# An attention and feed-forward kernel: one buffer for squares and sums, sums of weights made over three chunks, and a matmul of zeros in each product visit

## The chip, the cores and the metric

One core of a Trainium2 chip runs the whole program. The metric is the time on the device in microseconds. The engines are named as in the profile: PE is TensorE's matmuls and PEld its weight loads, DVE is VectorE, ACT is ScalarE, POOL is GpSimd, SP issues DMAs.

## The reference

Attention with a window and with block summaries, then a feed-forward layer with a squared relu. Sizes: batch 4, 8 heads, 768 positions, head size 64; 3072 tokens of 512 features, 2048 hidden features.

```python
def attn(q, k, v):                      # block = 32, window = 16
    k_sum = k.reshape(B, H, nb, block, D).max(axis=3)
    v_sum = v.reshape(B, H, nb, block, D).mean(axis=3)
    scores_l = scale * q @ k.T          # kept where |i - j| < window, else -1e9
    scores_s = scale * q @ k_sum.T + log(block)
    a = softmax(concat(scores_l, scores_s))
    return a @ concat(v, v_sum)

def ffn(x, w_in, w_out):                # x: attention output, (3072, 512)
    h = maximum(x @ w_in, 0)
    return (h * h) @ w_out
```

## The kernel before

The tokens are worked off in 12 chunks of 256. A list of tokens (`START`) orders the first two chunks and the preparation of the weights; from chunk 2 on `period` writes the order out, chunk by chunk, in 8 slots. The program is not reordered: each engine takes its instructions in the order in which they are issued.

Every matmul keeps float32 accuracy by splitting each operand into a high part, rounded to float32r, and a low part, the rest; a product is high x high + high x low + low x high, three matmuls. Weights are split once, activations as they come.

In slot n of chunk c PE runs `ffn1_pair`: the first layer for two blocks of 128 hidden features, 24 matmuls of 128 x 256 into one PSUM bank `ph`. Then it runs `second` for the slot before: the second layer for the four 128 x 128 blocks of squares. While PE does that and the next slot's first layer, the other engines turn `ph` into squares and their high and low parts, `gh` and `gl` (two buffers, by slot parity). So PE comes back to a slot's squares one first layer and one second layer after their bank is full.

From chunk 3 on, seven of the eight pairs use a product scheme with 7 instead of 8 block products (`products`, 21 matmuls of 128 x 256; a plain visit, as for pair 0 and in chunk 2, is 12 of 128 x 512). It needs sums of blocks of squares (`squares_and_sums`: four differences on VectorE, L443 to L449) and sums of blocks of `w_out`, made once (`build`, in five steps: six additions on GpSimd over four steps, then two casts on ScalarE and two subtractions on VectorE). The sums of pairs 1, 3, 5 and 7 don't fit: they are written to DRAM and read back a little before each use (`stream`). Four PSUM banks gather the products; `open_banks` starts them with matmuls of zeros, and `evict_products` adds them up at the chunk's end.

`BUILDS` says in which slot each step of a build is issued: "b" ahead of the slot's squares, "m" after them, "a" after the attention's middle part. In each slot L400 makes the relu on ScalarE, L406 squares three blocks there (high part, plain), L440 makes the product on VectorE in place, L447 the plain low part on GpSimd, L443, L448 and L449 the sums in a buffer of their own, L453 their high part on ScalarE and L454 their low part on GpSimd. In plain slots L411 and L414 do product and low part on VectorE.

Attention for the next chunk's two groups of 128 positions is laid over the slots: scores in slots 0 and 3, the masked maximum (`mask_max`), exponentials on ScalarE, `inverse` on VectorE and `norm` on GpSimd in slots 1, 2 and 4, 5, transposes (`turn`, L343, 12 a group) on VectorE in slots 2, 3 and 5, 6, outputs (L361, 64 matmuls) in slot 7. The second group's outputs need its last four transposes, which stand on VectorE behind slot 6's product and sums. Chunks 3, 4, 6 and 7 also carry the block sums of the next batch's K and V, chunks 2, 5 and 8 put the summary of V in place.

Of the kernel before, what the change touches and what calls it, by code (L numbers as in the profile page):

```python
# [11 lines left out]
F32 = mybir.dt.float32  # L12
# [12 lines left out]
P = 128  # L25
# [12 lines left out]
STREAMED = (1, 3, 5, 7)  # L38
BUILDS = {
# [40 lines left out]
def attn_ffn_kernel(ctx: ExitStack, tc: tile.TileContext, q, k, kt, v, vt, v0, w, masks, ident, mean, out):  # L80
# [24 lines left out]
    r_sb = const.tile([P, DM], F32, name="r")  # L105
    s_sb = const.tile([P, DM], F32, name="s")
# [189 lines left out]
    def mask_max(g, h):  # L296
# [4 lines left out]
        if half not in nmx:  # L301
            nmx[half] = work.tile([P, 4], F32, name="nmx", tag="nmx", bufs=7)
            sm[half] = work.tile([P, 4], F32, name="sm", tag="sm", bufs=7)
# [124 lines left out]
    def squares(ph, k):  # L428

        r = relu(ph, r_sb, nc.scalar)  # L430
        high_square(flat(gh_sb, k), r)
        square(ph, r)
        low_square(flat(gl_sb, k), ph, flat(gh_sb, k))

    def squares_and_sums(ph, k):

        r = relu(ph, r_sb, nc.scalar)
        o = slice(0, 3 * P)
        high_square(gh_sb[:, k, o], r[:, o])
        nc.vector.tensor_mul(out=r, in0=ph, in1=r)  # L440
        a12, a22, a11, a21 = (r[:, i * P : (i + 1) * P] for i in range(4))
        s1, s3, s2, s4 = (s_sb[:, i * P : (i + 1) * P] for i in range(4))
        nc.vector.tensor_sub(  # L443
            out=s_sb[:, 0 : 2 * P].rearrange("p (a b) -> p a b", a=2), in0=a21.unsqueeze(1).to_broadcast([P, 2, P]),
            in1=r[:, P : 3 * P].rearrange("p (a b) -> p a b", a=2),
        )
        nc.gpsimd.tensor_sub(out=gl_sb[:, k, o], in0=r[:, o], in1=gh_sb[:, k, o].bitcast(F32))  # L447
# [143 lines left out]
    def slot(c, n, before, mid, after, last):  # L591
# [29 lines left out]
        if summed:  # L621
            split_sums(k)
# [242 lines left out]
```

## Time and profile before

| | |
|---|---|
| median of 3 runs | 667.4 us (666.64 to 669.68) |
| the profiled execution | 667.81 us, its span 666.0 us |
| TensorE matmul, weight load | 609.5 us (92%), 567.6 us (85%) |
| VectorE | 510.1 us (77%) |
| ScalarE | 291.6 us (44%) |
| GpSimd | 277.9 us (42%) |
| mean granted TensorE clock | 0.974 of full speed |

The times of the rows are of the profiled execution and count from its span's start. The busy time of a matmul overlaps that of its neighbours, so a busy share says little of how fast they follow each other; starts do.

### The profile page before, as it was taken

To read this page: it belongs to the slowest core of one execution; us is meant where nothing else is said; L and a number is where in the kernel's file an instruction comes from. 1 tells how busy PE (TensorE), PEld (TensorE's weight loads), DVE (VectorE), ACT (ScalarE), POOL (GpSimd) and SP (SyncE) were. 2 spreads that over 40 slices of the span, in tenths; PEclk is the share of its full clock that TensorE was granted. 3 is DMA by queue.
4 is the path that set the end of the run, shared out by engine and by line. 5 is a ranking of instruction groups with operands and counts; after the bars stand their busy time and mean duration, and the time that the engine had idled before them with its cause. 6 is when DMAs were issued, how large, how long until landed. Compare 5 with 4: busy or idle time off the path is not lost.

```text
span 666.0 us, 14839 instructions
## 1 busy us (share of the span) xinstructions
PE 609.5 (92%) x5859; PEld 567.6 (85%) x5859; DVE 510.1 (77%) x1240; ACT 291.6 (44%) x748; POOL 277.9 (42%) x252
## 2 busy tenths in 40 slices
PE   3689999999989788998999998998998999999997
PEld 2578888988878788998988998988998998998897
DVE  4898998957756876787787788788698588588554
ACT  3678685224444333443443443443434444443232
POOL 3635462005637662442453343343254244244242
PEclk9789999999989977999999999998999999999999
DMA  8689311550216421732621732732532432331410
GB/s 337 215 351 376 116 64 48 184 189 1 88 58 200 171 96 65 237 111 96 215 88 48 238 112 96 230 120 74 186 104 83 138 132 82 127 97 48 155 67 33
DMA packets 27638, 91.15 MB, mean 137 GB/s; under 512 B 3376, under 2 KB 3504, under 8 KB 25520
## 3 DMA queue, kind: packets, MB, share of 16 engines
q1 hardware_dynamic: 27568, 90.20, 39.2%
q8 instruction: 46, 0.75, 0.5%
q14 instruction: 24, 0.20, 0.1%
HBM read 80.75 MB, written 9.44 MB: 135 GB/s over the span
## 4 chain that ended last, share of the span: by engine, by line
PE 39%; DVE 38%; ACT 12%; issue 5%; POOL 4%; DMA 1%; DVEq 0%; SPq 0%; ACTq 0%; POOLq 0%
PE ph L392 17%; DVE pT L343 8%; DVE s L443 8%; PE zw L522 6%; ACT e_sb L312 5%; DVE r L440 4%; PE o_ps L463 4%; PE o_ps L522 4%; PE o_ps L586 3%; ACT r L400 2%; DVE s L448 2%; DVE s L449 2%; ACT gh L406 2%; DVE e_sb L304 2%; DVE w_sb L263 1%
## 5 line engine op out<-in xcount | busy, mean ns | idle before, releaser
L392 PE MATMUL ph<-xh,w_sb 128*128 128x256 f32 x1408 | 251.9, 281 | 2.0 <-DVE gl L414 1.1
L392 PEld LDWEIGHTS ph<-xh,w_sb 128*128 128x128 f32 x1408 | 215.9, 189 | 8.2 <-issue 2.7
L392 PE MATMUL ph<-xl,w_sb 128*128 128x256 f32 x704 | 197.1, 280 | 0.2
L392 PEld LDWEIGHTS ph<-xl,w_sb 128*128 128x128 f32 x704 | 132.8, 189 | 1.6 <-DVE xl L377 1.6
L447 POOL TENSOR_TENSOR gl<-r,gh 128x384 fp32r<-128x384 f32 x63 | 64.5, 1024 | 150.4 <-DVE r L440 145.7
L453 ACT CAST gh<-s 128x512 fp32r<-128x512 f32 x63 | 39.1, 621 | 181.2 <-DVE s L449 171.6
L454 POOL TENSOR_TENSOR gl<-s,gh 128x512 fp32r<-128x512 f32 x63 | 81.9, 1300 | 76.2 <-issue 58.4
L343 DVE STREAM_TRANSPOSE pT<-e_sb 32x256 f32<-32x256 f32 x228 | 99.4, 436 | 3.3
L400 ACT ACTIVATE r<-ph 128x512 f32<-128x512 f32 x85 | 50.3, 592 | 84.1 <-PE ph L392 36.7
L312 ACT ACTIVATE e_sb<-e_sb,nmx 128x120 f32<-128x120 f32 x192 | 73.5, 384 | 25.9 <-DVE nmx L304 25.9
L330 POOL TENSOR_TENSOR e_sb<-e_sb,sm 128x480 f32<-128x480 f32 x43 | 43.3, 1008 | 96.2 <-DVE sm L325 88.6
L443 DVE TENSOR_TENSOR s<-r 128x256 f32<-128x256 f32 x63 | 75.4, 1197 | 6.5
L440 DVE TENSOR_TENSOR r<-ph,r 128x512 f32<-128x512 f32 x63 | 43.5, 691 | 37.5 <-ACT gh L406 30.3
L406 ACT ACTIVATE gh<-r 128x384 fp32r<-128x384 f32 (+1 forms) x96 | 54.0, 562 | 20.5 <-PE o_ps L463 12.9
L522 PE MATMUL zw<-sums,gh 128*128 128x256 f32 x252 | 51.5, 286 | 0.7 <-ACT gh L453 0.6
L522 PE MATMUL zw<-w_sb,gh 128*128 128x256 f32 x252 | 51.7, 287 | 0.3 <-ACT gh L406 0.3
L522 PE MATMUL o_ps<-w_sb,gh 128*128 128x256 f32 x252 | 50.3, 281 | 0.0
L256 POOL TENSOR_TENSOR w_raw<-w_raw 128x1024 int32<-128x1024 int32 x16 | 34.2, 2147 | 37.0 <-DVE w_raw L251 13.9
L304 DVE CUSTOM_DVE_ANT_0 e_sb<-s_ps,mask_sb 128x120 f32<-128x120 f32 x192 | 42.6, 274 | 8.2 <-PE s_ps L292 5.8
L586 PE MATMUL o_ps<-w_sb,gh 128*128 128x512 f32 x144 | 46.1, 402 | 0.2 <-ACT gh L406 0.2
L411 DVE TENSOR_TENSOR ph<-ph,r 128x512 f32<-128x512 f32 x25 | 17.4, 695 | 33.6 <-ACT r L400 33.3
L522 PEld LDWEIGHTS zw<-sums,gh 128*128 128x128 f32 x252 | 39.5, 194 | 2.0 <-ACT gh L453 2.0
(119 smaller groups left out, 1165.4 us busy)
## 6 DMA issues: line engine op xcount, KB each, us to landing
sums<-sums SPq DMA_DIRECT2D x40, 768.0 KB, 4.8
w_raw<-in_w SPq DMA_DIRECT2D x16, 1024.0 KB, 10.2
v_sb<-in_v SPq DMA_DIRECT2D x24, 384.0 KB, 6.7
k_sb<-in_k SPq DMA_DIRECT2D x18, 384.0 KB, 5.4
q_sb<-in_q SPq DMA_DIRECT2D x24, 256.0 KB, 5.5
out<-ob SPq DMA_DIRECT2D x22, 256.0 KB, 2.1
kv<-in_kt SPq DMA_DIRECT2D x8, 384.0 KB, 3.2
kv_sb<-in_kt SPq DMA_DIRECT2D x8, 384.0 KB, 4.0
```

The source lines that it names most:

```text
L304: nc.vector.tensor_tensor_reduce(out=e_sb[:, h, 0:NK], in0=s_ps[g][h % 2][:, h // 2, 0:NK], in1=m, scale=-scale, scalar=3.0e38, op0=ALU.ad ...
L312: nc.scalar.activation(e, e, AF.Exp, bias=nmx[half][:, i : i + 1], scale=-1.0, accum_out=sm[half][:, i : i + 1])
L343: nc.vector.transpose(out=pT[g % 2][j * 32 : j * 32 + 32, :, i * 32 : i * 32 + 32], in_=e_sb[i * 32 : i * 32 + 32, :, j * 32 : j * 32 + 32],)
L392: nc.tensor.matmul(ph, lhsT=w_sb[f][:, w, cc * P : (cc + 1) * P], rhs=x[c][:, cc, :], start=(n == 0), stop=(n == 3 * NC4 - 1))
L400: nc.scalar.activation(r, ph, AF.Relu)
L406: nc.scalar.activation(gh, r, AF.Square)
L440: nc.vector.tensor_mul(out=r, in0=ph, in1=r)
L443: nc.vector.tensor_sub(out=s_sb[:, 0 : 2 * P].rearrange("p (a b) -> p a b", a=2), in0=a21.unsqueeze(1).to_broadcast([P, 2, P]), in1=r[:, P ...
L447: nc.gpsimd.tensor_sub(out=gl_sb[:, k, o], in0=r[:, o], in1=gh_sb[:, k, o].bitcast(F32))
L454: nc.gpsimd.tensor_sub(out=gl_sb[:, k, o], in0=s_sb, in1=gh_sb[:, k, o].bitcast(F32))
L522: nc.tensor.matmul(bank[n_ps][:, o], lhsT=g_[:, k, blk * P : (blk + 1) * P], rhs=b[:, w], start=False, stop=(n == 2 and (n_ps, o.start) in ...
L586: nc.tensor.matmul((X, Y)[tt], lhsT=g_[tt], rhs=w_sb[2 * p + i][:, w, DM:], start=(begins and i == 0 and m == 0), stop=(ends and i == 1 an ...
```

## The change

Squares and sums share one buffer `r_sb` of seven blocks, and the relu has its own, `h_sb`. The product is no longer made in place: it writes four blocks of `r_sb`, with a gap for two sums. All seven blocks get their high part by one cast on ScalarE and their low part by one subtraction on GpSimd (`split`), issued after the middle part of the attention. The square on ScalarE and the plain low part go. Plain slots do the same with four blocks. The product visit first takes the 14 matmuls with high parts of squares, then the 7 with low parts, and begins with a matmul of zeros on 8 columns. The builds of the seven sums are issued over chunks 2 (pairs 1, 2, 3), 3 (5, 7) and 4 (4, 6), each with its last step ahead of the next slot's squares; pairs 4 and 6 stay plain in chunk 3. `nmx` has 6 buffers instead of 7, and the DMA scratch is 512 instead of 1024.

```diff
@@ -36,14 +36,14 @@
 FROM_KT = 6
 NP = NF // 2
 STREAMED = (1, 3, 5, 7)
+PRODUCTS_FROM = {1: 3, 2: 3, 3: 3, 5: 3, 7: 3, 4: 4, 6: 4}
 BUILDS = {
-    2: [(2, "a", 1, 0), (2, "a", 1, 1), (3, "b", 1, 2), (3, "b", 1, 3), (3, "a", 1, 4)]
-    + [(4, "b", 2, 0), (4, "b", 2, 1), (4, "a", 2, 2), (4, "a", 2, 3), (5, "b", 2, 4)]
-    + [(5, "a", 3, 0), (5, "a", 3, 1), (6, "b", 3, 2), (6, "b", 3, 3), (6, "a", 3, 4)]
-    + [(7, "b", 4, 0), (7, "b", 4, 1), (7, "a", 4, 2), (7, "a", 4, 3)],
-    3: [(0, "b", 4, 4), (0, "a", 5, 0), (0, "a", 5, 1), (0, "a", 5, 2), (0, "a", 5, 3), (1, "a", 5, 4)]
-    + [(2, "b", 7, 0), (2, "b", 7, 1), (3, "b", 7, 2), (3, "b", 7, 3), (3, "a", 7, 4)]
-    + [(4, "b", 6, 0), (4, "b", 6, 1), (5, "b", 6, 2), (5, "b", 6, 3), (5, "a", 6, 4)],
+    c: [(n, "a", p, step) for p, at in pairs for step, n in enumerate(at)] + [(at[3] + 1, "b", p, 4) for p, at in pairs]
+    for c, pairs in {
+        2: ((1, (1, 1, 2, 2)), (2, (3, 3, 4, 4)), (3, (5, 5, 6, 6))),
+        3: ((5, (1, 2, 2, 3)), (7, (4, 4, 5, 5))),
+        4: ((4, (1, 2, 2, 3)), (6, (4, 4, 5, 5))),
+    }.items()
 }
 LAST_ORDER = (2, 1, 4, 3, 6, 5, 7, 0)
 MASKED = -1.0e9
@@ -102,8 +102,8 @@
     pT = [const.tile([P, H, P], F32, name=f"pT{i}") for i in range(2)]
     ksums = [const.tile([P, NPAIR, NB], F32, name=f"ksum{i}") for i in range(2)]
     vsum = const.tile([P, NPAIR, 32], F32, name="vsum")
-    r_sb = const.tile([P, DM], F32, name="r")
-    s_sb = const.tile([P, DM], F32, name="s")
+    h_sb = const.tile([P, DM], F32, name="h")
+    r_sb = const.tile([P, 7 * P], F32, name="r")
     gh_sb = const.tile([P, 2, 7 * P], F32R, name="gh")
     gl_sb = const.tile([P, 2, 7 * P], F32R, name="gl")
     xh_sb = const.tile([P, NPAIR, CT], F32R, name="xh")
@@ -299,7 +299,7 @@
         m = mask_sb[:, 0 if t == 0 else 2 if t == NT - 1 else 1, :]
         half, i = divmod(h, 4)
         if half not in nmx:
-            nmx[half] = work.tile([P, 4], F32, name="nmx", tag="nmx", bufs=7)
+            nmx[half] = work.tile([P, 4], F32, name="nmx", tag="nmx", bufs=6)
             sm[half] = work.tile([P, 4], F32, name="sm", tag="sm", bufs=7)
         nc.vector.tensor_tensor_reduce(
             out=e_sb[:, h, 0:NK], in0=s_ps[g][h % 2][:, h // 2, 0:NK], in1=m, scale=-scale, scalar=3.0e38,
@@ -427,31 +427,27 @@
 
     def squares(ph, k):
 
-        r = relu(ph, r_sb, nc.scalar)
-        high_square(flat(gh_sb, k), r)
-        square(ph, r)
-        low_square(flat(gl_sb, k), ph, flat(gh_sb, k))
+        h = relu(ph, h_sb, nc.scalar)
+        nc.vector.tensor_mul(out=r_sb[:, 0:DM], in0=ph, in1=h)
+        return lambda: split(k, DM)
 
     def squares_and_sums(ph, k):
 
-        r = relu(ph, r_sb, nc.scalar)
-        o = slice(0, 3 * P)
-        high_square(gh_sb[:, k, o], r[:, o])
-        nc.vector.tensor_mul(out=r, in0=ph, in1=r)
-        a12, a22, a11, a21 = (r[:, i * P : (i + 1) * P] for i in range(4))
-        s1, s3, s2, s4 = (s_sb[:, i * P : (i + 1) * P] for i in range(4))
-        nc.vector.tensor_sub(
-            out=s_sb[:, 0 : 2 * P].rearrange("p (a b) -> p a b", a=2), in0=a21.unsqueeze(1).to_broadcast([P, 2, P]),
-            in1=r[:, P : 3 * P].rearrange("p (a b) -> p a b", a=2),
+        h = relu(ph, h_sb, nc.scalar)
+        r = r_sb.rearrange("p (a b) -> p a b", b=P)
+        nc.vector.tensor_mul(
+            out=r_sb[:, 0 : 6 * P].rearrange("p (a b) -> p a b", a=2)[:, :, 0:CT],
+            in0=ph.rearrange("p (a b) -> p a b", a=2), in1=h.rearrange("p (a b) -> p a b", a=2),
         )
-        nc.gpsimd.tensor_sub(out=gl_sb[:, k, o], in0=r[:, o], in1=gh_sb[:, k, o].bitcast(F32))
-        nc.vector.tensor_sub(out=s2, in0=a11, in1=s1)
-        nc.vector.tensor_sub(out=s4, in0=a12, in1=s2)
-
-    def split_sums(k):
-        o = slice(3 * P, 7 * P)
-        nc.scalar.copy(out=gh_sb[:, k, o], in_=s_sb)
-        nc.gpsimd.tensor_sub(out=gl_sb[:, k, o], in0=s_sb, in1=gh_sb[:, k, o].bitcast(F32))
+        nc.vector.tensor_sub(out=r[:, 2:5:2], in0=r[:, 4:5].to_broadcast([P, 2, P]), in1=r[:, 1:4:2])
+        nc.vector.tensor_sub(out=r[:, 5], in0=r[:, 3], in1=r[:, 2])
+        nc.vector.tensor_sub(out=r[:, 6], in0=r[:, 0], in1=r[:, 5])
+        return lambda: split(k, 7 * P)
+
+    def split(k, n):
+        gh = gh_sb[:, k, 0:n]
+        nc.scalar.copy(out=gh, in_=r_sb[:, 0:n])
+        nc.gpsimd.tensor_sub(out=gl_sb[:, k, 0:n], in0=r_sb[:, 0:n], in1=gh.bitcast(F32))
 
     X, Y, Z, W = bank[6], bank[7], bank[2], bank[3]
 
@@ -470,7 +466,7 @@
         return [[g_[:, k, b * P : (b + 1) * P] for b in FIRST[i]] for g_ in (gh_sb, gl_sb)]
 
 
-    built, sums = set(), {}
+    sums = {}
     dram = {p: tc.dram_tile([P, 1536], F32, name=f"sums{p}") for p in STREAMED}
 
     def halves(f, m):
@@ -502,7 +498,6 @@
         nc.vector.tensor_sub(out=b12[:, 1], in0=t1, in1=b12[:, 0].bitcast(F32))
         if p in STREAMED:
             nc.sync.dma_start(out=dram[p].rearrange("p (h c) -> p h c", h=2), in_=t.bitcast(F32))
-        built.add(p)
 
     def stream(p, tag_room=True):
         t = room(F32R, "sums")[:, 0:1536] if tag_room else shared(F32R, "sums")
@@ -514,10 +509,13 @@
         t3, t4, t2 = (sums[p][:, :, i * CT : (i + 1) * CT] for i in range(3))
         t1, b11, b21, b22 = halves(2 * p, 1), halves(2 * p, 0), halves(2 * p + 1, 0), halves(2 * p + 1, 1)
         lo, hi = slice(0, CT), slice(CT, DM)
-        plain = (2, b11, 2, lo), (0, b21, 6, lo), (1, t4, 7, lo)
-        summed = (4, t3, 3, lo), (3, t1, 3, hi), (5, t2, 2, hi), (6, b22, 6, hi)
-        passes = [(m, n) for m in plain for n in range(3)] + [(m, n) for m in summed for n in range(2)]
-        for (blk, b, n_ps, o), n in passes + [(m, 2) for m in summed]:
+        plain = (3, b11, 2, lo), (0, b21, 6, lo), (1, t4, 7, lo)
+        summed = (4, t3, 3, lo), (2, t1, 3, hi), (5, t2, 2, hi), (6, b22, 6, hi)
+        passes = [(m, n) for ms in (plain, summed) for m in ms for n in range(2)]
+        nc.tensor.matmul(
+            Z[:, 0:8], lhsT=zero.to_broadcast([P, P]), rhs=zero.to_broadcast([P, 8]), start=False, stop=False
+        )
+        for (blk, b, n_ps, o), n in passes + [(m, 2) for m in plain + summed]:
             g_, w = ((gh_sb, 0), (gh_sb, 1), (gl_sb, 0))[n]
             nc.tensor.matmul(
                 bank[n_ps][:, o], lhsT=g_[:, k, blk * P : (blk + 1) * P], rhs=b[:, w],
@@ -569,15 +567,20 @@
     def order(c):
         return LAST_ORDER if c == n_c - 1 else range(NP)
 
+    def in_products(c, p):
+        return c >= PRODUCTS_FROM.get(p, n_c)
+
     def second(c, n):
 
         p, k = order(c)[n], n % 2
         begins, ends = n == 0, n == NP - 1
-        summed = c > 2
-        if summed and begins:
+        if begins and c > 2:
             open_banks(*((Z, W) if p == 0 else (X, Y, Z, W)))
-        if p in built:
-            products(p, k, ((2, CT), (3, CT), (6, CT), (7, 0)) if ends else ((2, CT), (3, CT)) if n == NP - 2 and c == n_c - 1 else ())
+        if in_products(c, p):
+            closes = ((6, CT), (7, 0)) if ends else ()
+            if not any(in_products(c, later) for later in list(order(c))[n + 1 :]):
+                closes += ((2, CT), (3, CT))
+            products(p, k, closes)
             return
         for tt in range(TPC):
             for i in range(2):
@@ -604,8 +607,7 @@
             scores(a + 1, 0, NPAIR)
         for do in before:
             do()
-        summed = c > 2 and p > 0
-        (squares_and_sums if summed else squares)(ph, k)
+        rest = (squares_and_sums if in_products(c, p) else squares)(ph, k)
         if n == NP - 1 and a < n_g:
             for g in (a, a + 1):
                 high_x(g)
@@ -618,8 +620,7 @@
                 evict(c - 1, NF - 1, tt, nc.scalar)
         for do in mid:
             do()
-        if summed:
-            split_sums(k)
+        rest()
         for do in after:
             do()
         for do in last:
@@ -631,14 +632,12 @@
         before, mid, after, last = steps = [[[] for _ in range(8)] for _ in range(4)]
         for n, where, p, step in BUILDS.get(c, ()):
             steps["bmal".index(where)][n].append(lambda p=p, step=step: build(p, step))
-        if c > 2:
-            last[0].append(lambda: stream(1))
-            last[2].append(lambda: stream(3))
-            last[4].append(lambda: stream(5))
-            if c < n_c - 1:
-                last[6].append(lambda: stream(7))
-            else:
-                last[1].append(lambda: stream(7, False))
+        for p in STREAMED:
+            if in_products(c, p):
+                if c == n_c - 1 and p == 7:
+                    last[1].append(lambda: stream(7, False))
+                else:
+                    last[p - 1].append(lambda p=p: stream(p))
         a = 2 * c + 2
         b, t = divmod(a, NT)
         if a >= n_g:
@@ -761,7 +760,7 @@
             o = FIRST[j][0] * P
             ffn1(c, 2 * f + j, ph_of[i][:, o : o + CT])
         elif op == "RE":
-            r_of[i] = relu(ph_of[i], r_sb, eng)
+            r_of[i] = relu(ph_of[i], h_sb, eng)
         elif op == "SQ":
             g_of[i] = [high_square(flat(gh_sb, i % 2), r_of[i])]
         elif op == "MU":
@@ -852,7 +851,7 @@
     arrays["masks"] = _masks()
     arrays["ident"] = np.eye(P, dtype=np.float32)
     arrays["mean"] = _mean()
-    nc = bacc.Bacc("TRN2", target_bir_lowering=False, num_devices=1, dynamic_dma_scratch_size=1024)
+    nc = bacc.Bacc("TRN2", target_bir_lowering=False, num_devices=1, dynamic_dma_scratch_size=512)
     args = [
         nc.dram_tensor(f"in_{n}", a.shape, mybir.dt.from_np(a.dtype), kind="ExternalInput").ap()
         for n, a in arrays.items()
```

## Rows read from the trace of the kernel before

**Rows 1.** Windows by chunk: us, length, busy of each engine, clock, DMA share, GB/s.

```profile
202.98:266.72 63.74, 54.36 (x483) 50.91 (x482) 49.09 (x107) 24.24 (x66) 35.46 (x35) 0.89 0.37 130
266.72:318.92 52.20, 48.89 (x484) 46.30 (x482) 42.35 (x109) 21.18 (x60) 19.99 (x18) 1.00 0.42 142
318.92:370.30 51.38, 49.39 (x484) 46.29 (x482) 40.66 (x109) 21.04 (x60) 21.95 (x21) 1.00 0.35 114
370.30:421.25 50.95, 48.16 (x483) 46.00 (x482) 41.43 (x107) 21.15 (x60) 19.96 (x18) 1.00 0.43 146
421.25:474.20 52.95, 49.69 (x483) 47.38 (x482) 42.34 (x109) 21.18 (x60) 19.97 (x18) 0.97 0.41 140
...
525.58:574.61 49.03, 47.90 (x483) 45.83 (x482) 38.62 (x103) 21.04 (x60) 20.00 (x18) 1.00 0.37 119
574.61:623.67 49.06, 47.00 (x451) 45.00 (x449) 38.50 (x101) 21.86 (x61) 22.29 (x20) 1.00 0.28 89
```

**Rows 2.** Order of time on PE, chunk 10: start, length, line, count, idle.

```profile
608.20 1.15 PE L361 MATMUL ph<-pT,v_sb 128*64 128x64 f32 x32
609.18 0.64 PE L361 MATMUL s_ps<-pT,v_sb 128*64 128x64 f32 x16
610.79 0.69 PE L361 MATMUL s_ps<-pT,v_sb 128*64 128x64 f32 x16 [0.98 <-DVE pT L343]
```

**Rows 3.** Order of time, other engines, slots 6 and 7 of chunk 10.

```profile
606.19 0.69 DVE L440 TENSOR_TENSOR r<-ph,r 128x512 f32<-128x512 f32 x1
...
606.96 1.02 POOL L447 TENSOR_TENSOR gl<-r,gh 128x384 fp32r<-128x384 f32 x1 [2.21 <-DVE r L440]
...
606.98 1.27 DVE L443 TENSOR_TENSOR s<-r 128x256 f32<-128x256 f32 x1
...
608.62 0.29 DVE L449 TENSOR_TENSOR s<-r,s 128x128 f32<-128x128 f32 x1
608.94 1.80 DVE L343 STREAM_TRANSPOSE pT<-e_sb 32x256 f32<-32x256 f32 x4
608.94 0.62 ACT L453 CAST gh<-s 128x512 fp32r<-128x512 f32 x1 [4.56 <-DVE s L449]
...
609.69 1.27 POOL L454 TENSOR_TENSOR gl<-s,gh 128x512 fp32r<-128x512 f32 x1 [1.72 <-issue]
```

**Rows 4.** The order of time on DVE in chunk 3.

```profile
237.32 0.43 DVE L443 TENSOR_TENSOR s<-r 128x256 f32<-128x256 f32 x1
```

**Rows 5.** Waits of PE in chunk 3: total us, times, longest.

```profile
PE zw L522 <- POOL gl L447: 4.5, 2, 2.7
```

**Rows 6.** Groups by shape, whole span: busy us, mean ns, idle before.

```profile
L330 POOL TENSOR_TENSOR e_sb<-e_sb,sm 128x480 f32<-128x480 f32 x43 | 43.3, 1008 | 96.2 <-DVE sm L325 88.6 <-ACT r L400 7.2 <-ACT gh L406 0.4
...
L487 POOL TENSOR_TENSOR ob<-w_sb 128x512 f32<-128x512 f32 x14 | 18.1, 1315 | 15.5 <-DMA out<-ob 8.3 <-DVE w_sb L502 7.0 <-POOL ob L487 0.2
...
L263 POOL TENSOR_TENSOR w_sb<-w_raw,w_sb 128x1024 fp32r<-128x1024 f32 x3 | 7.6, 2535 | 2.4 <-ACT w_sb L137 2.3
...
L200 DVE TENSOR_REDUCE vsum<-kv_sb 128x24 f32<-128x768 f32 x8 | 7.5, 937 | 0.1
...
L499 ACT CAST sums<-ob 128x768 fp32r<-128x768 f32 x7 | 5.8, 833 | 12.1 <-POOL ob L495 12.1
```

**Rows 7.** Windows of PE: two runs of 24 matmuls in chunk 11.

```profile
627.96:630.69 2.73, 2.73 (x26) 1.00 0.85 249
633.07:635.90 2.83, 2.83 (x26) 1.00 0.82 341
```

**Rows 8.** Waits of PE in chunk 2.

```profile
PE s_ps L361 <- DVE pT L343: 2.7, 1, 2.7
```

**Rows 9.** DMA issues of the page: count, KB each, us to landing.

```profile
sums<-sums SPq DMA_DIRECT2D x40, 768.0 KB, 4.8
```

**Rows 10.** Weight loads by line: count, minimum, median, maximum ns.

```profile
L522 PEld LDWEIGHTS zw<-w_sb,gh x252: 186/188/337, 208.8 to 658.0; 128*128 128x128 f32 x126
...
L361 PEld LDWEIGHTS ph<-pT,v_sb x352: 132/138/138, 44.0 to 609.1; 128*64 128x64 f32 x176
```

## The prediction

> **What bounds the kernel now.** I read the windows by chunk first [rows 1]: from chunk 3 on each row is the stretch between two first uses of the opened banks, with the busy time of each engine. The reader is to see that TensorE is busy for nearly all of it, and that chunks doing the same matmuls still differ: 49.0 us for chunks 9 and 10, 51 to 53 for 5 to 8 (chunk 8 as chunk 5), 63.7 for chunk 3. What differs is waiting, so the question is who is waited for. Then the order of time on TensorE at the end of chunk 10 [rows 2]: of the 64 matmuls of the two attention outputs 48 run, and the last 16 sit 0.98 us until VectorE's transposes `pT` are there; from the step of the matmuls before it, the next one would have come 1.2 us earlier. This wait is in every chunk with attention. Then VectorE, ScalarE and GpSimd at that moment [rows 3]: VectorE goes without a pause from the product of one slot to its four transposes, and its broadcast subtraction (L443) takes 1.27 us. Its engine is not slow: in chunk 3 the same instruction takes 0.43 us [rows 4]. At 606.96 GpSimd's L447 begins, at 606.98 L443 does, and it ends one subtraction's length after GpSimd's end: it stood behind GpSimd for 0.84 us. So in the attention half of a chunk VectorE sets the end, TensorE elsewhere, and in chunk 3 GpSimd, whose sums of weights hold up the low parts (4.5 us in two waits, [rows 5]).
>
> **The change, part by part.** My unit is a slot; T is the end of its first-layer matmuls.
>
> *VectorE's relief.* L447 disappears. GpSimd's one subtraction now waits for the cast, the cast for the last of VectorE's three, so the three meet no subtraction of their own slot; and they can't meet that of the slot before, because the product writes the buffer which it reads and so waits for its end. L443 falls from 1.27 to 0.43 us. The product also no longer waits for ScalarE's square, since it doesn't overwrite what the square reads.
>
> The Trainium skill, "SBUF — State Buffer", section "Who interferes with whom", says that a VectorE instruction with two SBUF inputs and a GpSimd instruction that reads SBUF exclude each other for a whole instruction. The 1.27 against 0.43 agrees with that. By this rule a 2.15 us subtraction is also a longer block than the 1.0 us one was for whatever still meets it.
>
> What still meets it is the first operation of the softmax inverse, in slots 2 and 5; I take that in below.
>
> *The new ring.* Product, subtractions, cast, GpSimd, next product follow each other through one buffer. Product to next instruction 0.79 (606.19 to 606.98); the first subtraction 0.43 and a gap of 0.03; from its end at 608.25 to the end of the last 0.66, less that gap: 1.88 [rows 3, 4]. Cast of 896: 512 take 0.62 [rows 3], 768 take 0.833 [rows 6], so 0.94; I take 0.95. From the cast's end to GpSimd 0.13 [rows 3]. GpSimd's 896: by the step from 384 to 512 (1.02 to 1.27, [rows 3]) 2.02; by the line from 512 to 1024 (1.315 and 2.535, [rows 6]) 2.23; I take 2.15, between them. With 0.13 for two semaphores the ring is 5.23 us. TensorE's bare slot is 24 and 21 matmuls at 0.114 us [rows 7], 5.12, with the 22nd 5.22. They are level: the ring costs nothing where it is 5.23 and 0.1 us a bare slot where it is 5.33. Bare slots are four in each of chunks 5 to 10 and seven in the last, 31.
>
> *The chunk that results.* Slot 4: relu done at T+0.85, product T+0.95, sums T+2.8, cast to T+3.8; GpSimd's normalization (1.0 us, [rows 6]) goes first, its subtraction ends at T+6.5, and TensorE wants the low parts at 5.22 for the slot and 15 matmuls more, T+6.9. Slot 5: the inverse waits for GpSimd (0.4), sums at T+8.95, cast to T+9.95 (wanted T+10.4), subtraction to T+12.2 (wanted T+12.2, no slack left), eight transposes to T+12.5. Slot 6: sums T+14.4, four transposes (1.80, [rows 3]) T+16.2; TensorE reaches the 49th output matmul at T+16.5. The 1.2 us wait is gone: 49.05 becomes 47.85. With the sum of V in slot 5 of chunks 6 and 7 (0.94 us on VectorE, [rows 6], and some 0.3 with its scaling) 0.8 us stay: 48.6. Where V is placed (chunks 5 and 8) I take 48.1. Six chunks: 2 x 47.85 + 2 x 48.6 + 2 x 48.1 = 289.1 against 304.75 [rows 1]: **-15.7 us**. Chunk 7's 53.0 holds a spell of the half clock after its waits (0.97 mean granted clock, [rows 1]); I let it go with them.
>
> *Sums of weights.* A build is two adds of 1.315 [rows 6] and four of half as many elements, some 5.5 us of GpSimd, then two casts on ScalarE (768 elements 0.833, 256 by the same step 0.4) and two VectorE operations. Chunk 3 had nearly three, chunk 4 none; now both have two, behind the slot's subtraction instead of ahead of it. But the casts stand ahead of the next relu on ScalarE, and wait for GpSimd's last add. In slot 4 this puts the relu some 3.7 us late, and everything queued behind it: 3.4 us until the cast, 0.9 for the low part. Slot 5, with two adds, a normalization and 2.15 on GpSimd: 1.3 and 0.5. Slot 6, relu late again: the first outputs wait 2.6 for a bank, the last 1.9 for transposes. Together 10.6 us a chunk, and about 2 for the clock that falls in such waits (0.89 mean in chunk 3, [rows 1]). Chunk 3 also makes two visits plain, 0.4 each. 2 x (47.85 + 10.6 + 2) + 0.8 = 121.7 against 115.9: **+5.8 us**. Bounds: at the old chunk 3's price, 14.7 over 49.0 for three builds, it would be near 0 or below, -4 if spreading helps; with chunk 3's waits in both, +11. Chunk 2 had 3.7 us of waits, 2.7 of them for transposes [rows 8], and a clock spell of 1; its three builds now cost 3.9 by the same reckoning. Its low part moves from VectorE to GpSimd (1.3), at T+3.8 where it is wanted at T+5.9, so it costs nothing alone, and what it would cost behind an add is in the 3.9: **-0.8**. The DMAs of the sums move with them; at 4.8 us from issue to landing [rows 9] for the write and again for the read, group 7's come back some 2 us before chunk 4 uses them, group 5's about when slot 6 does; SP's loads of q, k and v stand behind them, a chunk ahead of their use.
>
> *Last chunk.* Its opening of banks waits for VectorE's evictions, which come 1.2 us sooner; its end waits longer, because the last plain visit has product, cast and GpSimd (1.3) in a row instead of a square beside a product, +1.5: **+0.3**.
>
> *The 22nd matmul.* Eight columns, so its price is the weight load of 128 columns. A load of 128 columns shows 188 ns, one of 64 shows 138 [rows 10]: 50 ns for 64, about 0.1 us for 128. From 0 (if it hides in a wait) to 0.114, a full step; I take 0.105, for 61 visits: 6.4. What it can return: the same 24 matmuls take 2.73 us in one slot and 2.83 in the next [rows 7], 0.114 or 0.118 a step, and in undisturbed stretches the step changes with each visit of 21, as if it went by whether the number of matmuls so far is even. In chunk 2, whose visits have 12, it is always the fast one. 1230 of 3003 recorded matmuls in chunks 3 to 11 are slow; with 22 all could be fast: 1230 x 0.0044 = 5.4 us. Net **+1.0**.
>
> Sum: -15.7 + 5.8 - 0.8 + 0.3 + 1.0 = -9.4. The profiled execution took 667.8 us (its span 666.0, 1.8 around it), the median of the runs is 667.4; so **658 us**.
>
> **Rivals.** *The step doesn't follow the count.* Waits inside visits already shift it, against the rule; then the zeros cost 6.4 and return nothing: 663.5. If all stay slow, 7 us more. 0.13. *Spreading the sums pays* (-4 instead of +5.8): 648. For it: the waits of rows 5 come from adds ahead of a low part, and adds now stand behind it. 0.14. *The relief is hidden:* normalization or inverse behind 2.15 us of GpSimd makes the transposes as late as today; six times 1.2 come back, 665. Against it: 0.3 us in slot 6 by my times. 0.09. *The ring sets the slot, and the kernel is slower:* the wait of the product for GpSimd. Each 0.1 us over 5.23 costs 31 x 0.1 = 3.1; at 5.53 the gain is gone, from 5.64 on it is slower than before by over 0.5%; with the subtractions still 0.84 longer, in their new strided form or behind other GpSimd work, it is 6.1 and 684. Against it: nothing of GpSimd is left to meet them in a bare slot. 0.09, middle 674.
>
> **How the numbers follow.** My forecast has 0.55, and 652 to 664 as its own range (the bounds of GpSimd's 896, 0.1 us on 31 slots, and of the zeros). The range of 646 to 668 takes in the spread sums, the unpaid zeros and the hidden relief, and leaves the ring and a still better case out. Half a per cent, about what a measurement of this kernel tells from no change, is 3.3 us. Faster by more, below 664: 0.52 of the forecast's 0.55, 0.14, 0.08 of the zeros' 0.13, 0.01 elsewhere: 0.75. Within: 0.17, the hidden relief and the rest of the forecast and of the zeros, with some ring. Slower: 0.08, nearly all ring.
>
> **What would show it.** L443's successor at 0.43 us; no pause at the 49th output matmul in chunks 9 and 10, which last under 48.5 with the zeros; GpSimd's 896 at 2.0 to 2.25 and a product that starts just after it in the last chunk; 24 matmuls in 2.73 us everywhere; long relus' waits in slots 4 and 6 of chunks 3 and 4. Wrong if visits begin with a wait for the cast in bare slots, or if chunks 3 and 4 together leave 112 to 127 us.

## The result, and the profile after

The changed kernel takes 650.64 us, median of 4 runs (649.25 to 651.41), against 668.1 (666.64 to 669.68) beside it: ratio 0.9736 [0.9705, 0.9766]. Forecast were 658.0 and a gain of 9.4; measured is one of 17.5. The profiled span is 649.4 us, before 666.0.

The windows by chunk, cut as in [rows 1] where the banks are opened (chunks 3 to 11):

```profile
203.02:258.79 55.77, 51.58 (x471) 47.89 (x469) 39.09 (x98) 21.33 (x57) 29.45 (x24) 0.94 0.43 147
258.79:318.00 59.21, 50.78 (x490) 48.18 (x489) 42.49 (x112) 22.07 (x57) 31.15 (x24) 0.97 0.38 125
318.00:365.70 47.70, 47.70 (x491) 46.33 (x490) 35.05 (x108) 20.13 (x53) 21.71 (x15) 1.00 0.38 123
365.70:413.87 48.17, 48.13 (x491) 46.44 (x489) 36.17 (x106) 20.02 (x53) 19.98 (x12) 1.00 0.47 154
413.87:462.24 48.37, 48.33 (x491) 46.62 (x490) 36.59 (x108) 20.23 (x53) 20.00 (x12) 1.00 0.47 153
462.24:511.38 49.14, 48.03 (x490) 46.47 (x489) 35.04 (x108) 20.13 (x53) 21.73 (x15) 1.00 0.37 119
511.38:559.08 47.70, 47.70 (x491) 46.33 (x490) 33.33 (x102) 20.02 (x53) 20.01 (x12) 1.00 0.37 123
559.08:605.68 46.60, 46.60 (x458) 45.52 (x457) 33.29 (x101) 19.84 (x51) 20.16 (x12) 1.00 0.29 94
605.68:649.40 43.72, 38.85 (x316) 37.26 (x314) 14.72 (x33) 10.84 (x15) 14.67 (x8) 1.00 0.26 97
```

In chunks 5, 9 and 10 the length and the busy time of TensorE, the first two numbers behind the stretch, are equal: the profile shows no idle time of TensorE there. Chunks 5 to 10 take 287.7 us, before 304.75 [rows 1]: all of the gain (-17.1). Chunks 3 and 4 take 115.0 together, before 115.94: the work that made chunk 3 long is now in chunk 4 as well. The last chunk rises from 42.36 to 43.7, and chunk 3 begins at 203.0 as before.

What TensorE waited for in chunks 5 to 10 (total us, times, longest), first before, then after. Of the 1.5 us for `ob` 0.6 lie behind the end of chunk 10, so the waits before are 12.2 us. The one wait after is in chunk 8:

```profile
PE s_ps L361 <- DVE pT L343: 8.1, 6, 2.1
PE zw L522 <- POOL gl L454: 3.0, 6, 0.8
PE o_ps L531 <- DVE ob L560: 1.5, 2, 0.9
PE zw L522 <- ACT gh L453: 0.2, 1, 0.2
```

```profile
PE o_ps L520 <- DMA sums<-sums: 1.1, 1, 1.1
```

The order of time on VectorE and on TensorE at the end of chunk 10, to set against [rows 2, 3]:

```profile
588.95 0.69 DVE L438 TENSOR_TENSOR r<-ph,h 128x512 f32<-128x512 f32 x1
589.68 0.43 DVE L442 TENSOR_TENSOR r<-r 128x256 f32<-128x256 f32 x1
590.14 0.29 DVE L443 TENSOR_TENSOR r<-r 128x128 f32<-128x128 f32 x1
590.46 0.29 DVE L444 TENSOR_TENSOR r<-r 128x128 f32<-128x128 f32 x1
590.78 1.80 DVE L343 STREAM_TRANSPOSE pT<-e_sb 32x256 f32<-32x256 f32 x4
...
592.92 1.15 PE L361 MATMUL ph<-pT,v_sb 128*64 128x64 f32 x32
593.90 1.10 PE L361 MATMUL s_ps<-pT,v_sb 128*64 128x64 f32 x32
594.94 0.27 PE L515 MATMUL zw<-zero 128*128 128x8 f32 x1
```

The broadcast subtraction takes 0.43 us, not 1.27; the transposes end at 592.58, before the first output matmul; all 64 run without the 0.98 us pause.

The ring, GpSimd to product, in the last chunk (start, length):

```profile
627.19 2.12 POOL L450 TENSOR_TENSOR gl<-r,gh 128x896 fp32r<-128x896 f32 x1 [3.20 <-ACT gh L449]
...
629.60 0.69 DVE L438 TENSOR_TENSOR r<-ph,h 128x512 f32<-128x512 f32 x1 [3.52 <-ACT h L400]
```

GpSimd's 896 elements end at 629.31, and the product begins 0.29 us later; it is the relu that it waited for: the ring does not set the slot.

### The profile page after: what moved, and what is told of

Read it like the earlier page. It is cut to its first block, busy times and chain, and to the rows that moved or that the text cites. A ratio compares the mean times of both kernels' runs of the same rounds, so it can differ in the third digit from the quotient of the medians.

```text
span 649.4 us, 14744 instructions
## 1 busy us (share of the span) xinstructions
PE 605.7 (93%) x5902; PEld 567.6 (87%) x5902; DVE 456.0 (70%) x1217; ACT 280.2 (43%) x685; POOL 285.8 (44%) x206
## 4 chain that ended last, share of the span: by engine, by line
PE 65%; DVE 14%; POOL 7%; ACT 6%; DMA 4%; issue 4%; SPq 0%; POOLq 0%; DVEq 0%; ACTq 0%
PE ph L392 29%; PE zw L520 11%; PE o_ps L520 8%; PE o_ps L589 5%; PE o_ps L459 4%; POOL gl L450 3%; DVE pT L343 2%; PE s_ps L277 2%; ACT e_sb L312 2%; DMA v_sb<-in_v 2%; PE ph L361 1%; DVE w_sb L263 1%; DMA sums<-sums 1%; PE zw L392 1%; ACT gh L449 1%
## 5 line engine op out<-in xcount | busy, mean ns | idle before, releaser
L450 POOL TENSOR_TENSOR gl<-r,gh 128x896 fp32r<-128x896 f32 (+1 forms) x80 | 153.7, 1922 | 221.4 <-ACT gh L449 206.8
L449 ACT CAST gh<-r 128x896 fp32r<-128x896 f32 (+1 forms) x80 | 69.3, 866 | 120.9 <-DVE r L444 101.2
L400 ACT ACTIVATE h<-ph 128x512 f32<-128x512 f32 x85 | 50.7, 597 | 125.9 <-PE ph L392 122.2
L438 DVE TENSOR_TENSOR r<-ph,h 128x512 f32<-128x512 f32 x61 | 42.1, 690 | 51.2 <-ACT h L400 40.1
L589 PE MATMUL o_ps<-w_sb,gh 128*128 128x512 f32 x160 | 51.8, 406 | 3.4 <-ACT gh L449 3.4
L520 PE MATMUL o_ps<-w_sb,gh 128*128 128x256 f32 x244 | 48.0, 278 | 0.0
L520 PE MATMUL zw<-sums,gh 128*128 128x256 f32 x244 | 47.9, 278 | 0.0
L322 DVE SCALAR_TENSOR_TENSOR sm<-sm 128x4 f32<-128x4 f32 x48 | 21.6, 449 | 27.4 <-ACT e_sb L312 27.3
L520 PEld LDWEIGHTS zw<-w_sb,gh 128*128 128x128 f32 x244 | 36.8, 189 | 4.2 <-ACT gh L449 4.1
L589 PEld LDWEIGHTS o_ps<-w_sb,gh 128*128 128x128 f32 x160 | 30.1, 194 | 9.9 <-ACT gh L449 4.0
L431 DVE TENSOR_TENSOR r<-ph,h 128x512 f32<-128x512 f32 x19 | 13.1, 688 | 36.3 <-ACT h L400 36.2
L459 PE MATMUL o_ps<-w_sb,gh 128*128 128x512 f32 x120 | 37.6, 394 | 0.0
```

Source lines behind the costliest of these rows:

```text
L400: nc.scalar.activation(r, ph, AF.Relu)
L438: nc.vector.tensor_mul(out=r_sb[:, 0 : 6 * P].rearrange("p (a b) -> p a b", a=2)[:, :, 0:CT], in0=ph.rearrange("p (a b) -> p a b", a=2), i ...
L449: nc.scalar.copy(out=gh, in_=r_sb[:, 0:n])
L450: nc.gpsimd.tensor_sub(out=gl_sb[:, k, 0:n], in0=r_sb[:, 0:n], in1=gh.bitcast(F32))
L459: nc.tensor.matmul((X, Y)[tt], lhsT=g_[tt], rhs=w_sb[f][:, w, DM:], start=(first and n == 0), stop=(last and n == 2),)
L520: nc.tensor.matmul(bank[n_ps][:, o], lhsT=g_[:, k, blk * P : (blk + 1) * P], rhs=b[:, w], start=False, stop=(n == 2 and (n_ps, o.start) in ...
```

## The experiments

Four questions: what the zeros do, what carries the gain of chunks 5 to 10, what the spread sums cost, and what is left. Each is timed against the kernel before; ratios are with 95% intervals. Times of chunks are of one profiled execution of each version.

**1 and 2. The zeros.** One version of the changed kernel drops the matmul, one gives it 256 columns.

```diff
-        nc.tensor.matmul(Z[:, 0:8], lhsT=zero..., rhs=zero.to_broadcast([P, 8]), ...)
```
```diff
-            Z[:, 0:8], lhsT=zero.to_broadcast([P, P]), rhs=zero.to_broadcast([P, 8]), ...
+            Z[:, 0:CT], lhsT=zero.to_broadcast([P, P]), rhs=zero.to_broadcast([P, CT]), ...
```

> The changed kernel without the matmul of zeros. Theory 1, from the trace of after (each visit 0.115 us longer, the step of the 24 matmuls still changing after every visit): the zeros cost a full step and return nothing, 61 x 0.115 = 7.0 us come back, 643.6 us. Theory 2, the net of my forecast (6.4 paid, 5.4 returned): 650 us, no difference that can be told from after's 650.6. Rival 3: the zeros fill a wait or keep the clock up: not faster than 650.6, and more half clock in the windows.

> The changed kernel with the matmul of zeros on 256 columns instead of 8. If the step (0.113 or 0.118 us) goes by whether the number of 256-column matmuls so far is even, 22 of them hold it at 0.113 in all undisturbed slots: some 5 us less than after, 645 to 646. If it changes with every product visit for another reason, nothing moves: 650.6 within 1, since the weight load already takes a full step.

Without zeros: 645.84 us, 0.9689 [0.9659, 0.972]; span 645.1, 4.3 less. With 256 columns: 653.28, 0.9809 [0.9771, 0.9846], so neither expectation of that run came. Two runs of 24 matmuls, one visit apart, in the last chunk (the length stands behind the stretch), changed kernel, then 256 columns:

```profile
625.81:628.64 2.83, 2.83 (x27) 1.00 0.00 0
631.22:633.95 2.73, 2.73 (x26) 1.00 0.02 6
```

```profile
626.52:629.35 2.83, 2.83 (x27) 1.00 0.00 0
631.92:634.75 2.83, 2.83 (x27) 1.00 0.02 6
```

With 8 columns the step still changes from visit to visit, as in [rows 7] and as without zeros. With 256 it holds through long stretches, but mostly at the slow level: from chunk 3 on 1975 of 2961 recorded matmuls start 116 to 120 ns after the one before, against 1340 in the changed kernel and 1325 without zeros (the count that gave 1230 of 3003 before). So a matmul of 8 columns does not stop the change and one of 256 mostly does. An even count is not the whole rule: in chunks 9 and 10 the first slot behind the plain visit, of 24 and 22, is fast, the next is slow, and only the slow step is then held. The price of the 8 columns is a full step: chunks 9 and 10, of seven product visits each, are 0.78 us shorter without them (47.69 to 46.91, 46.61 to 45.83), 0.11 a visit.

**3 and 5. The last step of a build ahead of the squares.** It holds the two casts which stand ahead of the next relu.

```diff
-    c: [(n, "a", p, step) ...] + [(at[3] + 1, "b", p, 4) for p, at in pairs]
+    c: [(n, "a", p, step) ...] + [(at[3] + 1, "a", p, 4) for p, at in pairs]
```
```diff
-    c: [(n, "a", p, step) ...] + [(at[3] + 1, "b", p, 4) for p, at in pairs]
+    c: [(at[3] + 1, "a", p, 4) for p, at in pairs] + [(n, "a", p, step) ...]
```

In the first the step stands behind the first adds of the build that begins in the same slot, which write over the buffer that it reads, so the weights' sums of four of the seven pairs (1, 2, 4, 5) are other ones, and the step's casts wait for those adds. In the second it goes first.

> The changed kernel with the last step of each build issued after the next slot's squares and cast instead of ahead of them; nothing else moves. Theory 1: what costs chunks 3 and 4 is the relu that stands on ScalarE behind casts which wait for GpSimd's adds: chunk 4 falls from 59.2 to 51 to 53 us and chunk 3 from 55.8 to 51 to 53, 639 to 643 us. Rival: GpSimd's queue itself (adds, normalization and the 2.1 us subtraction) is late: at most 2 us less, 648.5 or more.

> The changed kernel with the last step of each build behind the slot's squares and cast, as in the run before of that kind, but now ahead of the next build's first step, so that no sum is overwritten before it is read. Theory 1 (the relu behind the casts is what costs chunks 3 and 4): these fall from 55.8 and 59.2 us to 51 to 54 each, 640 to 645 us. Rival (GpSimd's queue is late, and the order on ScalarE only names the waiter): 648 to 652, with waits of the product visits for the low part in the place of those for the cast.

The first: 654.98, 0.9827 [0.9797, 0.9857], slower than the changed kernel; since its casts wait for other adds, it does not test the place of the step. The second: 643.87, 0.9637 [0.9606, 0.9667], 6.8 below it, but not where expected: chunk 3 begins 4.3 us earlier (198.7), chunk 3 is 1.8 shorter, chunk 4 only 0.9 (58.27). There the wait moved. Waits of TensorE in chunk 4, and VectorE's order of time:

```profile
PE s_ps L361 <- DVE pT L343: 4.6, 1, 4.6
PE o_ps L520 <- DVE sums L497: 1.8, 1, 1.8
```

```profile
292.61 2.20 DVE L497 TENSOR_TENSOR sums<-ob,sums 128x768 fp32r<-128x768 f32 x1 [1.79 <-ACT sums L495]
294.73 0.41 DVE L498 TENSOR_TENSOR w_sb<-ob,w_sb 128x256 fp32r<-128x256 f32 x1
295.15 1.80 DVE L343 STREAM_TRANSPOSE pT<-e_sb 32x256 f32<-32x256 f32 x4
```

The four transposes stand behind the step's own VectorE instruction, which first waits 1.79 us for the cast and then takes 2.20 (mean of seven in the changed kernel 0.98): GpSimd's subtraction runs from 291.92 to 294.00, and it ends 0.81 behind that.

**4, 6 and 11. What carries the gain.** The kernel before, with each half of the relief alone and with both, and no common buffer, cast or zeros. *Low parts later* moves GpSimd's first subtraction behind the second and takes the low parts last in the visit; *own relu* gives the relu a buffer, in plain slots too (room: the gap tile, `nmx` and the DMA scratch are cut). The diffs are shortened:

```diff
 def squares_and_sums(ph, k):
         ...
-        nc.gpsimd.tensor_sub(out=gl_sb[:, k, o], in0=r[:, o], in1=gh_sb[:, k, o].bitcast(F32))
         ...
 def split_sums(k):
         ...
+        o = slice(0, 3 * P)
+        nc.gpsimd.tensor_sub(out=gl_sb[:, k, o], in0=r_sb[:, o], in1=gh_sb[:, k, o].bitcast(F32))
         ...
-        passes = [(m, n) for m in plain for n in range(3)] + [(m, n) for m in summed for n in range(2)]
-        for (blk, b, n_ps, o), n in passes + [(m, 2) for m in summed]:
+        passes = [(m, n) for ms in (plain, summed) for m in ms for n in range(2)]
+        for (blk, b, n_ps, o), n in passes + [(m, 2) for m in summed + plain]:
```
```diff
-        r = relu(ph, r_sb, nc.scalar)
+        h = relu(ph, h_sb, nc.scalar)
+        r = r_sb
         ...
-        high_square(gh_sb[:, k, o], r[:, o])
-        nc.vector.tensor_mul(out=r, in0=ph, in1=r)
+        high_square(gh_sb[:, k, o], h[:, o])
+        nc.vector.tensor_mul(out=r, in0=ph, in1=h)
```

> The kernel before, with one thing of the change alone: the low part of the three plain blocks is issued on GpSimd behind that of the sums, so that it no longer runs beside VectorE's subtractions, and the product visit takes all low parts last. Buffers, square, casts, builds stay as they were. Theory 1, the collision on the way to SBUF is what the relief consists of: the first subtraction falls from 1.27 to 0.43 us, chunks 9 and 10 from 49.0 to 47.5 us, 652 to 658 us in all. Rival: the relief comes from the product no longer waiting for the square and from the single cast: less than 3 us, 665 to 668.

> The kernel before with the plain low part behind the sums' low part (as in the run that took 682 us) and a buffer of its own for the relu; a filler tile and the DMA scratch are cut to make room. In the first such run 53 relus waited for GpSimd's late subtraction, 108 us in all, since the product was made in the relu's buffer. Theory 1, collision and shared buffer together are the relief, the single cast and the single subtraction are not: 651 to 658 us, chunks 9 and 10 at 47 to 48 us. Rival: two subtractions of 1.3 and 1.0 us and a square on top are themselves too long for the slot: 662 us or more.

> The kernel before with the relu's own buffer alone; the plain low part stays beside VectorE's subtractions. With the run that moved the low part alone (682 us) and that with both (639) it makes the four corners. Theory 1, the subtraction's 0.84 us is the larger part of the relief: most of the waits stay, 660 to 666 us, and the first subtraction still takes 1.27. Rival: the product that no longer waits for the square gives VectorE 0.6 us a slot, nearly as much: 648 to 656.

| low parts later | own relu | us | ratio | chunks 5 to 10 |
|---|---|---|---|---|
| no | no (before) | 667.4 | | 304.75 |
| yes | no | 682.3 | 1.023 [1.0192, 1.0268] | 313.3 |
| no | yes | 652.88 | 0.978 [0.9751, 0.9809] | 293.2 |
| yes | yes | 638.86 | 0.9562 [0.9531, 0.9593] | 282.5 |

Low parts later alone is slower than before, which neither of its expectations had: the first subtraction is down to 0.42, and the next relu waits, since the late GpSimd instruction still reads the buffer that it writes. ScalarE's waits:

```profile
ACT r L400 <- POOL gl L455: 108.3, 53, 2.4
```

Own relu alone frees the product from the square but not the subtractions; its time is the one that the rival had. GpSimd and VectorE in chunk 10:

```profile
590.99 1.26 POOL L449 TENSOR_TENSOR gl<-r,gh 128x384 fp32r<-128x384 f32 x1 [2.27 <-DVE r L442]
```

```profile
590.95 0.43 DVE L445 TENSOR_TENSOR s<-r 128x256 f32<-128x256 f32 x1
591.40 0.99 DVE L450 TENSOR_TENSOR s<-r,s 128x128 f32<-128x128 f32 x1
592.43 0.29 DVE L451 TENSOR_TENSOR s<-r,s 128x128 f32<-128x128 f32 x1
```

VectorE now begins 0.04 us ahead of GpSimd, and it is the second subtraction that ends just behind it (0.99 instead of 0.29; over the whole run 0.964 in the mean). GpSimd's 384 elements, which begin second now, take 1.22 us in the mean of this run, 1.02 before: here GpSimd, too, pays for beginning second. Even so 11.5 us are gone from chunks 5 to 10, and 10.7 more go with the subtractions cleared. The 11.5 come from the product and not from the relu: in the kernel before, each relu of these chunks begins at least 0.55 us after the last reader of the shared buffer has ended, so none was held by it; the product began at least 0.64 us behind its relu, and in experiment 11 it begins as little as 0.10 behind. Both halves are needed, and are all: the version with both, with a square and a cast on ScalarE and two GpSimd instructions, has chunks 9 and 10 at 46.91 and 45.83, to the hundredth those of the changed kernel without zeros. The common buffer and its one cast are worth nothing there by themselves.

**7 and 8. Plain visits as before; builds as before.** Each is put back alone in the changed kernel.

```diff
 def squares(ph, k):
-        nc.vector.tensor_mul(out=r_sb[:, 0:DM], in0=ph, in1=h)
-        return lambda: split(k, DM)
+        high_square(flat(gh_sb, k), h)
+        square(ph, h)
+        low_square(flat(gl_sb, k), ph, flat(gh_sb, k))
+        return lambda: None
```
```diff
-PRODUCTS_FROM = {1: 3, 2: 3, 3: 3, 5: 3, 7: 3, 4: 4, 6: 4}
+PRODUCTS_FROM = {1: 3, 2: 3, 3: 3, 5: 3, 7: 3, 4: 3, 6: 3}
-    c: [(n, "a", p, step) for p, at in pairs ...
+    2: [(2, "a", 1, 0), (2, "a", 1, 1), (3, "b", 1, 2), ...
```

> The changed kernel with the plain visits (pair 0, chunk 2, pairs 4 and 6 in chunk 3) as before: square on ScalarE, product in place, low part on VectorE. My forecast took the new way for +1.5 us at the end of the last chunk and nothing elsewhere. By that the last chunk falls from 43.7 to 42.5 and chunk 2's two waits of about 1 us for the low part stay: 649 us. Rival: the plain low parts wait behind the builds on GpSimd, in chunk 2 and in chunk 3 (3.3 us at one visit): 644 to 647.

> The changed kernel with the builds in chunks 2 and 3 and in the slots of the kernel before, and all seven pairs as products from chunk 3 on. By the trace, chunks 3 and 4 together took 115.9 us before and 115.0 after, so the new places cost or gain little: chunk 4 falls to 48.5, chunk 3 rises to 64 to 68, 648 to 654 us in all. Rival, spreading is a good part of the gain (as one of my rivals had it): 656 us or more.

Plain visits as before: 647.28, 0.9683 [0.9648, 0.9718]; chunk 3 begins at 198.4, 4.6 us earlier, and the last chunk is 0.8 shorter (42.93). Builds as before: 650.18, 0.9731 [0.97, 0.9763], the changed kernel's time within its interval; chunks 3 and 4 take 62.85 and 48.21, 111.1 together instead of 115.0, but chunk 3 begins 2.7 later. This run puts back both the chunks of the builds and the places of their steps in the slot.

**9, 10 and 12. Putting it together.** 9 is the changed kernel without zeros, with the step of 5 and the plain visits of 7. 10 is 9 with the square, cast and two GpSimd instructions of 6, so against 6 it has the builds alone changed. 12 is 10 with the last step of three builds at the end of its slot, behind the transposes:

```diff
-    c: [(at[3] + 1, "a", p, 4) for p, at in pairs] + ...
+    c: [(at[3] + 1, "l" if p in (3, 6, 7) else "a", p, 4) for p, at in pairs] + ...
```

> The changed kernel without the zeros, with the last build step behind squares and cast, and with plain visits as before. From the three runs alone: spans 4.3 (no zeros), 7.5 (last step) and 6.0 (plain visits) below after's 649.4; the last two both remove chunk 2's 4.5, so 649.4 - 4.3 - 7.5 - 1.5 = 636. If the pieces don't add because a new wait appears in chunks 3 and 4: 640 to 644. The one buffer with one cast stays, so if chunks 9 and 10 stand at 46.9 and 45.8 here as in the run with two parts, that buffer itself is worth nothing there.

> The run with two parts and the relu's own buffer (638.9 us), with the change's builds over three chunks, the last step behind the squares. There chunks 2 to 4 end at 311.8 us; here, by the run with the last step moved (chunk 2 ends 4.3 earlier, chunks 3 and 4 take 112.3 with 1.4 of zeros in them), at 198.7 + 110.9 = 309.6, so 2 us less: 636 to 637. Rival: with low parts in two pieces, GpSimd's queue with the builds is no worse than with 2.1 us in one, and chunks 3 and 4 fall to 105 or less: 631 to 633.

> The two parts with the spread builds (633.6 us), with the last step of the last build of chunks 2, 3 and 4 issued at the slot's end, behind the four transposes. In chunk 4 the outputs waited 4.9 us for transposes that stood on VectorE behind that step's subtraction, which waits for a cast and for GpSimd. Theory 1, place on VectorE is the cost: chunk 4 falls from 58.5 to 53 to 54 us, 627 to 629 in all. Rival, the transposes are late by the sums themselves, and the step only shifts them: less than 1.5 us, 632 or more.

9 takes 634.05 (633.33 to 634.78), 0.9495 [0.9472, 0.9517]. 10 takes 633.64, 0.949 [0.9467, 0.9512], the same as 9, and 5.2 below 6: with the last step behind the squares, the builds of the change do pay, and by the windows they pay in chunk 2 (chunk 3 begins at 197.09, in 6 at 202.26; chunks 3 and 4 together take 109.8, in 6 109.6). 12 takes 629.27 (628.43 to 630.25), 0.9427 [0.9402, 0.9452], 21 us below the changed kernel and the best of all. Waits of TensorE for the transposes in chunk 4, 10 and then 12:

```profile
PE s_ps L362 <- DVE pT L344: 4.9, 1, 4.9
```

```profile
PE s_ps L362 <- DVE pT L344: 1.0, 1, 1.0
```

Chunk 4 falls from 58.49 to 54.19 us, nearly the whole of the 4.8 that the span falls: the wait was the transposes' place in VectorE's queue.

## Why the prediction was right, and where its sum was off

**VectorE's relief: mechanism right, size too small.** The subtraction fell to 0.43 us and the wait at the 49th output matmul is gone. The Trainium skill, "SBUF — State Buffer", section "Who interferes with whom", says that a VectorE instruction with two SBUF inputs and a GpSimd one that reads SBUF shut each other out. Experiment 11, where the loss moves to whichever subtraction meets GpSimd (0.99 against 0.29), agrees. One reading in the working was off: L443 ends 0.27 us after GpSimd (608.25 and 607.98 in [rows 3]), not one subtraction's length of 0.43. The 0.84 us that it lost stands.

The size came out too small because the working took chunk 9, less the 1.2 us at the outputs, as the base of all six chunks. Chunks 5 to 10 gave -17.1 with 42 matmuls of zeros in them, and -21.1 in the run without (283.64 us), where -15.7 was forecast. Chunk 9 itself fell by 2.1 without zeros (49.03 to 46.91), not by 1.2. The starts of the matmuls in the two traces, before and without zeros, tell what the base left out. The outputs give back 9.4 us in the six chunks. Pauses inside the product visits, where a matmul starts more than a step after the one before, give 9.6; only 3.2 of such pauses are among the waits listed above, the others are shorter and lie in time that counts as busy. Pauses in the first layer give 1.2, the opening of the last chunk's banks 1.1; slower steps take 0.2 back. Of the 9.6 some 1.5 lie in the spell of half clock in chunk 7 (461.6 to 465.1 us, granted clock 0.51, behind a wait of 2.1 for transposes), which the changed kernel does not have. The part that the working named and put at nothing is the product freed from the square: by experiment 11 it is 11.5 us of these chunks, half of the relief.

**The ring: right.** From the product at 624.27 in the last chunk to GpSimd's end at 629.31 are 5.04 us (0.69, 0.43, 0.29, 0.29, 0.94 and 2.12 with their gaps), where the working has 5.11 without the step to the next product. GpSimd is done 0.29 us before that product, which waits for the relu; the rival needed a ring of 5.33 to cost anything.

**The 22nd matmul: price right, return wrong.** Forecast +6.4 and -5.4. Its price is 0.11 a visit where TensorE does not wait, and it returned nothing, as the step still changed with each visit. So the rival in which the zeros are paid and return nothing holds in this one term. All 61 would be some 7 us; in the run without zeros the span falls by 4.3, since chunks 3, 4, 6 and 7, with 26 of the visits, together do not get shorter (55.77 to 55.73, 59.21 to 59.38, 48.17 to 48.05, 48.37 to 48.51): there other waits fill what is freed. Making the count even is no remedy either: where the step was held, it was mostly slow.

**Sums of weights: waits right, sum wrong.** Forecast +5.8, measured -1.0, and -0.8 in the run without zeros. In chunk 4 the late relus came as described: GpSimd's last add, then the two casts, then the relu, on GpSimd and on ScalarE (times of slot 4):

```profile
278.56 0.74 POOL L491 TENSOR_TENSOR ob<-ob 128x256 f32<-128x256 f32 x1
```

```profile
279.33 0.83 ACT L495 CAST sums<-ob 128x768 fp32r<-128x768 f32 x1 [3.75 <-POOL ob L491]
280.07 0.40 ACT L496 CAST w_sb<-ob 128x256 fp32r<-128x256 f32 x1
280.38 0.59 ACT L400 ACTIVATE h<-ph 128x512 f32<-128x512 f32 x1
```

And TensorE's waits in that chunk:

```profile
PE zw L520 <- ACT gh L449: 4.0, 2, 3.0
PE ph L361 <- DVE r L438: 3.0, 1, 3.0
PE zw L520 <- POOL gl L450: 0.9, 2, 0.6
PE ph L392 <- DVE xl L377: 0.4, 1, 0.4
```

They make 8.3 us where 10.6 was forecast. By the mean granted clock, (1 - 0.97) x 59.2 and (1 - 0.94) x 55.8, the clock cost at most 1.8 and 3.3 us, where I took 2 each. Two other terms were off: the chunk under the waits (46.9 where I had 47.85, 1.9 for two), and chunk 3, whose waits come to 4.1 where 10.6 were forecast; 3.3 of them are at one plain visit, at 228.13 us. Its slots 4 and 6 are the plain ones; that this is why builds cost less there was not tested. As the change has them, the builds neither pay nor cost (experiment 8), so the rival in which they pay did not come. That is not a verdict on spreading, since the chunks of the builds and the places of their steps changed together. The last step moved behind the squares is worth 6.8 us (experiment 5); with it there the builds of the change gain 5.2 on the old ones (10 against 6); and behind the transposes it is worth 4.4 more (12). What costs is the queue in which the last step stands.

**Plain visits and chunk 2: wrong.** -0.8 was forecast and nothing came. The sentence that the low part on GpSimd costs nothing alone failed: with the plain visits as before (experiment 7), chunk 3 begins 4.6 us earlier. TensorE's waits in chunk 2 of the changed kernel:

```profile
PE o_ps L589 <- ACT gh L449: 1.6, 2, 1.2
PE o_ps L589 <- POOL gl L450: 1.3, 2, 0.7
PE ph L392 <- ACT gh L449: 1.1, 1, 1.1
```

The working priced the low part and left out the high part: the cast now stands behind the product, where the square came right behind the relu (relu at 177.66 and cast at 179.68 in one slot; in experiment 7 relu at 175.55, square at 176.17). GpSimd's low parts also stand ahead of its adds, for which the step's casts wait (that slot's first cast starts at 176.61, in experiment 7 at 174.50). The place of the last step costs about as much (4.3, experiment 5); with both put back the gain is 5.9 (chunk 3 at 197.1), so they overlap.

**Last chunk: near.** Forecast +0.3, measured +1.3, of which 0.6 go without the zeros. 0.5 is the last plain visit's wait for GpSimd, which is gone in 7.

By the terms, taken from the run without zeros: -21.1 for the six chunks, -0.8 for the sums, +0.2 up to chunk 3, +0.8 at the end and +4.3 for the zeros make the 16.6 by which the span fell. The relief is 5.4 us and the sums are 6.6 better than forecast, both on the same side, and the zeros took back 3.3 of it. So that the time lies well inside the range of 646 to 668 is partly luck: the errors partly cancel, and without the zeros the kernel takes 645.84, just below the range.

Not tried: the changed kernel's one buffer with the step placement of 12; and no run held the fast step from chunk 3 on, so why the step has two levels, and what chooses the one that is held, stays open.

## What to carry to other kernels

When an edit frees two waits of one instruction, price both: the buffer that lets the product go ahead of the square was worth as much as the subtraction's collision, and moving the low parts without it cost 15 us. A step of preparatory work is placed by what stands behind its instructions on each queue they touch: the same last step cost 6.8 us ahead of a relu and 4.4 ahead of four transposes, and least behind both. A filler matmul of 8 columns cost nearly as much as a step of 256 where TensorE did not wait, so it is tried by itself before it is put in 61 places. What is taken for a chunk's floor, here chunk 9 less its listed wait, may hold shorter pauses that no list of waits shows; the starts show them.

## What was not expected of the hardware

TensorE's step for 128x256 matmuls, with the granted clock at 1.00 throughout, has two levels, 0.113 and 0.118 us. With 24 and 21 such matmuls in turn it changes with each visit of 21; with 24 and 22 it was mostly held, at the slow level. A matmul of 8 columns in front of the 21 costs 0.11 us, nearly a step of one with 256, and the step changes as without it.
